# GeGLU feed-forward by seven block products: the order of the first loads and the shape of the last block

## Chip, cores and metric

The kernel runs on one core of one Trainium2 chip. The metric is device time in microseconds (us) of one execution. Three runs of the kernel before gave 272.92, 273.94 and 274.2 us; the median is 273.94. "Line" and L284 are lines of the kernel before unless said otherwise. TensorE (PE) does matmuls, with its weight loads shown apart (PEld); DVE, ACT and POOL are the vector, scalar and GpSimd engines; SP only issues DMAs and ACT issues some too (SPq and ACTq in the profile).

## The reference

```python
B, S, D, F = 32, 32, 1024, 3584
def reference(x, w_gate, w_up, w_down):
    return (_gelu(x @ w_gate) * (x @ w_up)) @ w_down
```

All inputs and the output are bf16; x is 1024 tokens by 1024 columns once its first two dimensions are flattened. `_gelu` is the tanh approximation.

## The kernel before, in words

Both matrix products are done on 2 x 2 blocks with seven block products instead of eight: sums and differences of blocks (s1 to s4 of the weights, t1 to t4 of x) are formed on POOL and DVE, multiplied on TensorE and combined. Tokens are split in two halves of 512 (NB), columns of x in two halves of four 128-wide pieces (KD = 4), columns of the gate and up weights in 28 pieces of 128 that are taken two at a time.

One of the seven products needs no sum: rows 512 to 1023 of w_gate (called `a12`) times the second column half of x for the first 512 tokens (`b21`, which has those x columns on partitions and the tokens along the row). The kernel begins with it, for 24 weight pieces "ahead", because it needs few bytes. `a12_ahead[i]` holds four weight pieces of group i, for the four 128-row steps k; `product_ahead` (line 284) multiplies one weight piece by `b21[:, k, cols]`, and its results wait in PSUM banks, for i = 0 in banks "CCAA".

The first x data does not come transposed. `load_nat` (line 197) loads x as it lies in memory, 128 tokens at a time, into `x_nat`: for column piece dt = 0 by SP's queue, for dt = 1 by ACT's queue. `transposed(dt)` (lines 260 to 267) makes four 128 x 128 transposes on TensorE (line 264), two to a PSUM tile, and DVE copies each pair to `b21` (line 267). Column pieces 2 and 3 come by a transposing DMA (`load_xT`, line 218). Gate rows k = 0 and k = 1 of group 0 come by SP's queue, one DMA each (line 211); those of group 1 by ACT's queue. Ahead of ACT's first load stands a tiny DMA `probe` (line 207) that nothing reads.

All of this is in a hand-written order (`manual_schedule`): every engine and every DMA queue works in program order. TensorE begins with six warm-up matmuls on constants (NWARM, line 256), then the four transposes of dt = 0, then products of k = 0 with the first 256 tokens, then `transposed(1)`, then k = 0 with the second 256 tokens, then k = 1 with both, then group 1:

```python
for k in range(KQ):                       # KQ = 2
    for half in range(2):
        for j in range(KB):               # KB = 4 weight pieces
            product_ahead(ps[0][j], 0, j, k, k + 1, slice(half * HALF * P, (half + 1) * HALF * P))
        if k == half == 0:
            transposed(1)
```

The second stage multiplies by w_down. Its products end with four stores of 128 rows (lines 577 to 581), after which one block is left: 128 tokens by 512 columns, the plain product of `a12_last` with `b21s` over 14 steps (HF). It is done as two blocks of 256 columns. Each is summed in a PSUM bank (line 588), added by DVE to `p1_last` (line 589) and stored by ACT's queue (line 590). The last of these stores ends the kernel.

Of the kernel before, what the change touches and what calls it, by code (L numbers as in the profile page):

```python
# [13 lines left out]
def kernel(  # L14
# [20 lines left out]
    nc = tc.nc  # L35
    P = nc.NUM_PARTITIONS
    fp32 = mybir.dt.float32
    f32r = mybir.dt.float32r
    bf16 = mybir.dt.bfloat16
# [4 lines left out]
    of = out.flatten_outer_dims()  # L44
    N, D = xf.shape
    F = w_gate.shape[1]
    NB = 512
    assert N == 2 * NB and D == 2 * NB and F % (4 * P) == 0
    DT, FT = D // P, F // P
    KD = DT // 2  # L50
# [4 lines left out]
    KQ = DT // 4  # L55
    HF = FT // 2
    MT = NB // P
    NWARM = 6
    KB = 4
    QF = HF // 2  # L60
    batches = [(0, KB), (KB, QF), (QF, QF + KB), (QF + KB, HF)]
# [2 lines left out]
    wg_r = w_gate.rearrange("(dt dp) f -> dp dt f", dp=P)  # L64
# [8 lines left out]
    xpool = one.enter_context(tc.tile_pool(name="x", bufs=1))  # L73
# [33 lines left out]
    def acc(tag):  # L107
        return ps1.tile([P, NB], fp32, name=f"ps{tag}", tag=tag, bufs=BANKS[tag])
# [5 lines left out]
    b21 = xpool.tile([P, KD, NB], bf16, name="b21")  # L114
# [72 lines left out]
    ones_w = nc.const_aps.tensor(1.0, [P, P], bf16)  # L187
    ones_m = nc.const_aps.tensor(1.0, [P, NB], bf16)
    ident = xpool.tile([P, P], bf16, name="ident")
    make_identity(nc, ident)  # L190
    NB_P = NB // P
    HALF = NB_P // 2
    x_nat = spool.tile([P, NB_P, KQ * P], bf16, name="x_nat", tag="s1")

    with tc.manual_schedule():
        def load_nat(eng, dt, p0, p1):
            eng.dma_start(  # L197
                out=x_nat[:, p0:p1, dt * P : (dt + 1) * P],
                in_=xf[p0 * P : p1 * P, (KD + dt) * P : (KD + dt + 1) * P].rearrange("(b p) d -> p b d", p=P),
            )  # L200

        assert KQ == 2
        load_nat(nc.sync, 0, 0, NB_P)


        probe = xpool.tile([P // 8, KQ, 2], bf16, name="probe")
        nc.scalar.dma_start(out=probe, in_=wg_r[::8, KD : KD + KQ, :2])

        def load_ahead(i, k0, k1, eng=nc.sync):
            f0 = i * KB  # L210
            eng.dma_start(
                out=a12_ahead[i][:, k0:k1, :],
                in_=wg_r[:, KD + k0 : KD + k1, f0 * P : (f0 + KB) * P],
            )

        def load_xT(nb, d0, d1):
            t = ((b11, b12), (b21, b22))[d0 // KD][nb]
            nc.sync.dma_start_transpose(
                out=t[:, d0 % KD : (d1 - 1) % KD + 1, :], in_=xf[nb * NB : (nb + 1) * NB, d0 * P : d1 * P]
            )  # L220

        load_ahead(0, 0, 1)
        load_nat(nc.scalar, 1, 0, NB_P)
        load_ahead(0, 1, 2)
        load_xT(0, KD + KQ, DT)
        load_ahead(1, 0, KQ, nc.scalar)
        a12_ahead += [spool.tile([P, KD, KB * P], bf16, name="a12b", tag=t) for t in ("s2", "s4", "s1", "s3")]
        for i in (0, 1):
            load_ahead(i, KQ, KD)
# [24 lines left out]
        warm_ps = acc("A")  # L254
        for _ in range(NWARM):
            nc.tensor.matmul(warm_ps, lhsT=ones_w, rhs=ones_m, start=True, stop=True)

        tps = [[ps1.tile([P, HALF * P], bf16, name="tp", tag="A", bufs=BANKS["A"]) for _ in range(2)] for _ in range(KQ)]

        def transposed(dt):  # L260
            for half, tp in enumerate(tps[dt]):
                p0 = half * HALF
                for b in range(HALF):
                    nc.tensor.transpose(  # L264
                        tp[:, b * P : (b + 1) * P], x_nat[:, p0 + b, dt * P : (dt + 1) * P], ident
                    )
                nc.vector.tensor_copy(b21[:, dt, p0 * P : (p0 + HALF) * P], tp)

        transposed(0)

        def prod(ps, lhs, rhs, start):
            for k in range(KD):
# [9 lines left out]
        def product_ahead(ps, i, j, k0=0, k1=KD, cols=slice(None)):  # L282
            for k in range(k0, k1):
                nc.tensor.matmul(  # L284
                    ps[:, cols],
                    lhsT=a12_ahead[i][:, k, j * P : (j + 1) * P],
                    rhs=b21[:, k, cols],
                    start=(k == 0 and not cols.start),
                    stop=(k == KD - 1),
                    skip_group_check=True,  # L290
                )
# [34 lines left out]
        ps = [[acc(t) for t in tags] for tags in ("CCAA", "AAAA")]  # L326
        for k in range(KQ):
            for half in range(2):
                for j in range(KB):
                    product_ahead(ps[0][j], 0, j, k, k + 1, slice(half * HALF * P, (half + 1) * HALF * P))  # L330
                if k == half == 0:
                    transposed(1)
        for j in range(KB):
            product_ahead(ps[1][j], 1, j, 0, KQ)
        for i in (0, 1):
# [28 lines left out]
        for ci in range(NCH):  # L364
# [8 lines left out]
            sn5, sn2, h1, h0 = [], [], [], []  # L373
# [17 lines left out]
            if fts[-1] < NAHEAD:  # L391
                h0 = first
# [184 lines left out]
        for m in range(MT):  # L577
            r0 = NB + m * P
            o = late.tile([P, NB], bf16, name="o_sb", tag="o_sb", bufs=2)
# [1 line left out]
            nc.scalar.dma_start(out=of[r0 : r0 + P, :NB], in_=o)  # L581

        o = late.tile([P, 2 * NB], bf16, name="o_last", tag="snb", bufs=MT)
        for h0 in range(0, NB, NB // 2):
            cols = slice(h0, h0 + NB // 2)
            ps = acc("C")[:, : NB // 2]
            for k in range(HF):
                nc.tensor.matmul(ps, lhsT=a12_last[:, k, :], rhs=b21s(k)[:, cols], start=(k == 0), stop=(k == HF - 1))  # L588
            tt(o[:, cols], p1_last[:, cols], ps, ADD)  # L589
            nc.scalar.dma_start(out=of[NB - P : NB, cols], in_=o[:, cols])  # L590
# [1 line left out]
_INS = ['x', 'w_gate', 'w_up', 'w_down']  # L592
_OUTS = [((32, 32, 1024), 'bfloat16')]
# [25 lines left out]
```

## Time and profile before

| what | value |
|---|---|
| median of three runs | 273.94 us |
| span of the profiled execution, first to last instruction | 272.0 us (272.05) |
| another time of the profiled execution | not given; the median is 1.89 us above its span |
| TensorE busy in the span | 267.1 us, 98% |
| first matmul of the warm-up | 0.78 us |
| first transpose of x / first product | 3.30 / 4.31 us |
| product of k = 1 begins | 6.28 us |
| last block: first matmul / last addition / end | 265.85 / 269.12 / 272.05 us |
| DMA, issue to landing: x_nat on SP / on ACT, 128 KB each | 2.5 / 3.2 us |
| probe / gate rows of 128 KB / of 256 KB on ACT | 2.1 / 3.0 and 4.4 / 4.6 us |
| stores of 128 KB / of 64 KB at the end | 1.7 / 1.6 us |

A row of the timeline has the start in us from the span's start, the duration, the engine with a "q" where its queue issues a DMA, the line, the operation, what it writes and reads, the shape, the number of instructions that the row merges, and in brackets the idle time before it with what ended it. A matmul's duration includes the time until its result is out, so that consecutive ones overlap: the pace is read from their starts.

### The profile page before, as it was taken

What the parts mean: (1) busy time and instruction counts of PE and PEld (TensorE: products, weight loads), DVE (VectorE), ACT (ScalarE), POOL (GpSimd) and SP (SyncE); (2) the same over time, 40 slices, a digit from 0 to 9 for tenths busy, and PEclk for the clock granted to TensorE, in tenths of its full rate; (3) what the DMA queues carried; (4) which work ended last, traced back from release to release, by engine and by line L of the source; (5) the groups of instructions that cost most, each with busy time, mean ns of one, the idle gap of its engine ahead of it and who ended that gap; (6) DMA issues with size and microseconds to landing.
All of it is one profiled execution on the core that took longest, in us unless ns stands there. A gap on an engine that the chain in (4) does not pass through costs nothing.

```text
span 272.0 us, 3399 instructions
## 1 busy us (share of the span) xinstructions
PE 267.1 (98%) x1199; PEld 193.4 (71%) x1212; DVE 201.2 (74%) x205; ACT 116.1 (43%) x189; POOL 119.3 (44%) x60
## 2 busy tenths in 40 slices
PE   8999999999999999999999999999999999999995
PEld 4444776886787688688688687764458888888884
DVE  1448998886976876876787458569999999997721
ACT  2335865545644643645636535434000307770000
POOL 1090099976995994994995978000000000000000
PEclk9999999999999999999999999999999999999999
DMA  7999130504505505415234290005981437855111
GB/s 174 323 227 281 39 99 17 158 25 130 154 2 154 154 4 154 128 27 157 69 88 118 50 319 17 0 2 182 356 273 60 158 112 253 276 187 174 54 61 58
DMA packets 56048, 35.86 MB, mean 132 GB/s; under 512 B 9824, under 2 KB 56032, under 8 KB 56032
## 3 DMA queue, kind: packets, MB, share of 16 engines
q1 hardware_dynamic: 52736, 33.17, 42.6%
q10 hardware_dynamic: 3296, 2.49, 2.9%
q8 instruction: 9, 0.15, 0.2%
q14 instruction: 7, 0.06, 0.1%
HBM read 31.72 MB, written 2.10 MB: 124 GB/s over the span
## 4 chain that ended last, share of the span: by engine, by line
PE 97%; DMA 1%; issue 0%; SPq 0%; DVE 0%
PE psA L273 38%; PE psA L425 24%; PE psC L273 19%; PE psC L425 7%; PE psA L284 5%; PE psC L284 3%; PE psC L588 1%; DMA a12a<-in_w_gate_dram 1%; SPq L197 0%; PE tp L264 0%; DVE o_last L589 0%
## 5 line engine op out<-in xcount | busy, mean ns | idle before, releaser
L273 PE MATMUL psA<-t,s 128*128 128x512 f32 x224 | 57.2, 397 | 0.0
L248 ACT ACTIVATE h<-c 128x512 bf16<-128x512 f32 x56 | 34.6, 631 | 41.6 <-DVE c L303 41.6
L273 PEld LDWEIGHTS psA<-t,s 128*128 128x128 f32 x224 | 42.1, 188 | 9.5
L170 POOL TENSOR_TENSOR s<-wu 128x1024 fp32r<-128x1024 bf16 x13 | 28.8, 2215 | 32.9 <-DMA wu<-in_w_up_dram 27.9
L171 POOL TENSOR_TENSOR s<-s,wg 128x1024 fp32r<-128x1024 f32 x14 | 31.7, 2263 | 15.0 <-DVE s L170 14.0
L173 POOL TENSOR_TENSOR s<-wg,wu 128x1024 fp32r<-128x1024 bf16 x13 | 28.4, 2188 | 0.0
L273 PE MATMUL psA<-b,wg 128*128 128x512 bf16 x119 | 27.8, 379 | 0.6
L273 PE MATMUL psA<-t,a22r 128*128 128x512 f32 x112 | 27.9, 391 | 0.0
L273 PE MATMUL psC<-t,s 128*128 128x512 f32 x112 | 27.9, 391 | 0.0
L273 PE MATMUL psC<-b22r,s 128*128 128x512 f32 x112 | 27.6, 389 | 0.0
L303 DVE TENSOR_TENSOR c<-sn,psA 128x512 f32<-128x512 f32 x32 | 21.8, 682 | 6.7 <-PE psA L273 5.7
L308 ACT COPY sn<-psC 128x512 f32<-128x512 f32 x28 | 16.4, 590 | 20.9 <-PE psC L273 15.2
L273 PEld LDWEIGHTS psC<-t,s 128*128 128x128 f32 x112 | 21.0, 188 | 4.5
L273 PEld LDWEIGHTS psA<-t,a22r 128*128 128x128 f32 x112 | 21.0, 188 | 4.5
L273 PEld LDWEIGHTS psC<-b22r,s 128*128 128x128 f32 x112 | 21.0, 188 | 4.4
L303 DVE TENSOR_TENSOR c<-sn,psC 128x512 f32<-128x512 f32 x28 | 19.2, 688 | 6.5 <-PE psC L273 6.5
L273 PEld LDWEIGHTS <-wg 128*128 128x128 bf16 x128 | 11.8, 98 | 15.3 <-issue 2.4
L172 POOL TENSOR_TENSOR s<-wg,s 128x1024 fp32r<-128x1024 bf16 x10 | 21.6, 2158 | 0.8
L402 DVE TENSOR_TENSOR lo<-c,h 128x512 bf16<-128x512 f32 x14 | 20.4, 1459 | 0.9
L308 ACT COPY sn<-psA 128x512 f32<-128x512 f32 x32 | 18.4, 592 | 6.1 <-PE psA L273 6.0
L303 DVE TENSOR_TENSOR c<-ahead,psA 128x512 f32<-128x512 f32 x24 | 16.4, 687 | 4.0 <-PE psA L273 2.4
L321 DVE TENSOR_TENSOR hi<-h,psA 128x512 bf16<-128x512 bf16 x14 | 9.6, 688 | 12.4 <-PE psA L273 12.4
(85 smaller groups left out, 381.0 us busy)
## 6 DMA issues: line engine op xcount, KB each, us to landing
wu<-in_w_up_dram SPq DMA_DIRECT2D x14, 512.0 KB, 4.0
wdb<-in_w_down_dram SPq DMA_DIRECT2D x12, 512.0 KB, 4.9
wg<-in_w_gate_dram SPq DMA_DIRECT2D x9, 512.0 KB, 5.2
wdb<-in_w_down_dram SPq DMA_DIRECT2D x12, 384.0 KB, 4.5
v<-in_w_down_dram SPq DMA_DIRECT2D x4, 512.0 KB, 6.4
out_dram<-o_sb ACTq DMA_DIRECT2D x15, 128.0 KB, 1.7
wg<-in_w_gate_dram SPq DMA_DIRECT2D x6, 256.0 KB, 4.6
v<-in_w_down_dram SPq DMA_DIRECT2D x4, 384.0 KB, 7.5
```

The lines of the kernel that those rows point to most:

```text
L170: yield engs[0].tensor_tensor(s1, a21, a22, ADD)
L171: yield engs[1].tensor_tensor(s2, s1, a11, SUB)
L172: yield engs[2].tensor_tensor(s4, a12, s2, SUB)
L173: yield engs[3].tensor_tensor(s3, a11, a21, SUB)
L248: nc.scalar.activation(h, src, ACT.Gelu_apprx_tanh)
L273: nc.tensor.matmul(ps, lhsT=lhs[:, k, :], rhs=rhs[:, k, :], start=(start and k == 0), stop=(k == KD - 1), skip_group_check=True,)
L284: nc.tensor.matmul(ps[:, cols], lhsT=a12_ahead[i][:, k, j * P : (j + 1) * P], rhs=b21[:, k, cols], start=(k == 0 and not cols.start), stop ...
L303: tt(t, s, ps, ADD)
L308: nc.scalar.copy(t, ps)
L321: tt(g_of(ft)[:, :NB], h0, psa, MUL)
L402: tt(g_of(ft)[:, NB:], added(sn5[fl], psa[fl]), h1[fl], MUL)
L425: nc.tensor.matmul(banks[m], lhsT=lhs(k)[:, m * P : (m + 1) * P], rhs=rhs(k), start=(start and k == 0), stop=(k == HF - 1), skip_group_che ...
```

## The change

At the start, x_nat for dt = 0 comes as two DMAs of two token blocks each, followed by dt = 1, all three on SP's queue. Gate rows k = 0 and k = 1 of group 0 go to ACT's queue, ahead of group 1's. The probe is gone. `transposed` now takes a half: only (0, 0) is done ahead of the first products; (0, 1), (1, 0) and (1, 1) follow them. There are five warm-up matmuls instead of six, and six small ones of 128 columns on constants (NFILL) behind the first two transposes.

At the end, the last block is done as 384 and 128 columns; the first is stored as before, and the second as two stores of 64 rows, one on ACT's and one on SP's queue.

```diff
-    NWARM = 6
+    NWARM = 5
+    NFILL = 6
...
-        load_nat(nc.sync, 0, 0, NB_P)
-        probe = xpool.tile([P // 8, KQ, 2], bf16, name="probe")
-        nc.scalar.dma_start(out=probe, in_=wg_r[::8, KD : KD + KQ, :2])
+        load_nat(nc.sync, 0, 0, HALF)
+        load_nat(nc.sync, 0, HALF, NB_P)
+        load_nat(nc.sync, 1, 0, NB_P)
...
-        load_ahead(0, 0, 1)
-        load_nat(nc.scalar, 1, 0, NB_P)
-        load_ahead(0, 1, 2)
+        for k in range(KQ):
+            load_ahead(0, k, k + 1, nc.scalar)
+        load_ahead(1, 0, KQ, nc.scalar)
         load_xT(0, KD + KQ, DT)
-        load_ahead(1, 0, KQ, nc.scalar)
...
-        def transposed(dt):
-            for half, tp in enumerate(tps[dt]):
-                p0 = half * HALF
-                for b in range(HALF):
-                    nc.tensor.transpose(
-                        tp[:, b * P : (b + 1) * P], x_nat[:, p0 + b, dt * P : (dt + 1) * P], ident
-                    )
-                nc.vector.tensor_copy(b21[:, dt, p0 * P : (p0 + HALF) * P], tp)
-
-        transposed(0)
+        def transposed(dt, half):
+            p0, tp = half * HALF, tps[dt][half]
+            for b in range(HALF):
+                nc.tensor.transpose(tp[:, b * P : (b + 1) * P], x_nat[:, p0 + b, dt * P : (dt + 1) * P], ident)
+            nc.vector.tensor_copy(b21[:, dt, p0 * P : (p0 + HALF) * P], tp)
+
+        transposed(0, 0)
+        for _ in range(NFILL):
+            nc.tensor.matmul(warm_ps[:, :P], lhsT=ones_w, rhs=ones_w, start=True, stop=True)
...
                 if k == half == 0:
-                    transposed(1)
+                    for dt, h in ((0, 1), (1, 0), (1, 1)):
+                        transposed(dt, h)
...
-        for h0 in range(0, NB, NB // 2):
-            cols = slice(h0, h0 + NB // 2)
-            ps = acc("C")[:, : NB // 2]
+        for h0, h1 in ((0, NB - P), (NB - P, NB)):
+            cols = slice(h0, h1)
+            ps = acc("C")[:, : h1 - h0]
             for k in range(HF):
                 nc.tensor.matmul(ps, lhsT=a12_last[:, k, :], rhs=b21s(k)[:, cols], start=(k == 0), stop=(k == HF - 1))
             tt(o[:, cols], p1_last[:, cols], ps, ADD)
-            nc.scalar.dma_start(out=of[NB - P : NB, cols], in_=o[:, cols])
+            if h1 < NB:
+                nc.scalar.dma_start(out=of[NB - P : NB, cols], in_=o[:, cols])
+                continue
+            for eng, r0 in ((nc.scalar, 0), (nc.sync, P // 2)):
+                eng.dma_start(
+                    out=of[NB - P + r0 : NB - P // 2 + r0, cols], in_=o[r0 : r0 + P // 2, cols]
+                )
```

## Prediction

> **What bounds the kernel now.** I read the busy table first, then the chain of waits, then the timeline of both ends. TensorE is busy 267.1 of 272.0 us, and the chain is TensorE for 97%.
>
> ```profile
> PE 267.1 (98%) x1199; PEld 193.4 (71%) x1212; DVE 201.2 (74%) x205; ACT 116.1 (43%) x189; POOL 119.3 (44%) x60
> ...
> PE 97%; DMA 1%; issue 0%; SPq 0%; DVE 0%
> ```
>
> The table by stretches says where the other 3% is: between 6.28 and 265.85 us TensorE's busy time falls short of the stretch by only 0.77 us (15.67 of 15.72, 37.83 of 38.00, 59.79 of 60.00, 59.76 of 60.00, 85.75 of 85.85, up to 265.85). So what is won or lost before 6.28 shifts all that follows, and what is won after 265.85 shortens the end. The change touches only these two stretches.
>
> The start, from the timeline (start, duration, engine, line; in brackets the idle time before it):
>
> ```profile
> 0.73 0.45 ACTq L207 DMA_DIRECT2D probe<-in_w_gate_dram  x1
> 0.74 0.45 SPq L197 DMA_DIRECT2D x_nat<-in_x_dram  x1
> 1.21 0.49 ACTq L197 DMA_DIRECT2D x_nat<-in_x_dram  x1
> 1.25 1.03 SPq L211 DMA_DIRECT2D a12a<-in_w_gate_dram  x2
> 1.73 0.53 ACTq L211 DMA_DIRECT2D a12a<-in_w_gate_dram  x1
> ...
> 3.30 0.62 PE L264 MATMUL tp<-ident,x_nat 128*128 128x128 bf16 x4
> 3.75 0.51 DVE L267 COPY b<-tp 128x256 bf16<-128x256 bf16 x2 [3.75 <-PE tp L264]
> 4.31 0.61 PE L284 MATMUL psC<-b,a12a 128*128 128x256 bf16 x2 [0.39 <-DMA a12a<-in_w_gate_dram]
> 5.14 0.63 PE L264 MATMUL tp<-ident,x_nat 128*128 128x128 bf16 x4
> 5.57 0.53 PE L284 MATMUL psC<-b,a12a 128*128 128x256 bf16 x2
> 6.28 0.39 PE L284 MATMUL psC<-b,a12a 128*128 128x256 bf16 x2
> ```
>
> Three waits can be seen: the first x piece (TensorE starts on it at 3.30), the first gate rows (0.39 us, until 4.31), and the second gate rows (the weight load at 6.28 waited 0.25 us, TensorE itself about 0.1). And the pace: warm-up weight loads start at 1.16, 1.58, 2.01, 2.44, that is 0.427 us for 512 columns; from 7.17 on 512 columns take 0.216 (32 in 7.07 us at 14.07). Narrow windows show the switch between 5.78 and 5.93. The granted-clock column reads 1.00 throughout, so the pace has to be read from the starts. I call it slow before about 5.86 and full after.
>
> The end:
>
> ```profile
> 265.85 3.23 PE L588 MATMUL psC<-wdb,a_last 128*128 128x256 bf16 x28
> 267.59 0.42 DVE L589 TENSOR_TENSOR o_last<-p_last,psC 128x256 bf16<-128x256 f32 x1 [2.44 <-PE psC L588]
> 268.05 1.87 ACTq L590 DMA_DIRECT2D out_dram<-o_last  x2
> 269.12 0.42 DVE L589 TENSOR_TENSOR o_last<-p_last,psC 128x256 bf16<-128x256 f32 x1 [1.11 <-PE psC L588]
> ```
>
> 28 matmuls, the last addition at 269.12, its store issued at 269.58, landed 1.6 us later (the rows of DMA issues), and then 0.8 us until the span ends, which the change does not touch.
>
> **The start, step by step.** Queues first. SP had x, gate row, gate row, transposed x; it gets x half, x half, x second piece, transposed x: four issues before and after, so its later loads keep their moments (the transposed x at 2.32). ACT had probe, x second piece, gate rows of the next group; it gets gate row, gate row, the same gate rows: again three, so its table load stays at 2.29. Only which bytes go first changes.
>
> (1) First x piece. 128 KB landed 2.5 us after issue (0.74 to 3.24); the probe, hardly any bytes, took 2.1. So 64 KB lands between 2.84 and 3.24; but now 128 KB of gate rows travels beside it, as beside the second x piece, which took 3.2: upper bound 3.94. I take 3.1, nearest to the first pair.
>
> (2) First gate row, issued at 0.73 rather than 1.25. It took 3.0 us then, so 3.7 at most; the wait of 0.39 us goes. What is late next is the transposed half. From the first transpose to the copy's start is 0.45 us (3.30 to 3.75), the copy itself 0.29, about 0.04 to TensorE: transposes at 3.14, half ready at 3.92. The six fillers are queued ahead on TensorE: two transposes and six fillers of 128 columns at 0.107 us (4 transposes: (0.63 - 0.31)/3) end at 3.14 + 8 x 0.107 = 4.00. So the first products start at 4.00 instead of 4.31: 0.31 us won, for now.
>
> (3) Four products of 256 columns at 0.213 end at 4.85. Then come six transposes where there were four: the second half's (0,1) was moved behind these products. End: 4.85 + 0.64 = 5.49. But the next products need (0,1)'s copy, a wait that was not there before (that copy was done at 4.25): 4.85 + 0.45 + 0.29 + 0.04 = 5.63. In the trace these products start at 5.57. So the 0.31 us is spent again: 0.10 on the two transposes and the rest of what it was ahead on the copy; queued behind that wait is all of TensorE.
>
> (4) From 5.63: two products at 0.213 and two at 0.109 (full pace past 5.86) end at about 6.20. The second gate row, issued at 1.21, takes at most the 4.4 us of its predecessor: 5.6, no wait. In the trace this point is 6.28. **Gain at the start: 0.08 us.** Ends: with x at 2.84 the point comes about 0.23 earlier; with x at 3.94 the new copy is ready at 6.47, and with four products at 0.109 the point is 6.9, 0.6 later.
>
> (5) The second x piece now is issued at 1.80 on SP, behind the two halves, instead of at 1.21. TensorE wants it at 4.85 + 0.21 = 5.06. By its own row (3.2 us) it lands at 5.0: no margin. The shortest of its size (2.5) gives 4.3. The longest is the gate row that had this very slot, issued at 1.80: 4.4 us, which gives 6.2. I take 5.0, since its company is what it was; at 6.2 TensorE would stand 1.2 us, the products begin at about 6.5 and end at 6.95: 0.65 us lost.
>
> The other loads: next group's gate rows, issued at 1.73 as before, landed at 6.3 and are wanted at 7.17; the transposed x landed at 7.2 and is wanted at 8.89. Covers of 0.9 and 1.7 us, if they slip; the change moves no byte in front of both queues together, only from one to the other. The missing probe and the one warm-up matmul fewer (0.43 us; TensorE then waits from 2.91 for x) cost nothing, as x is later than either.
>
> **The end.** The same 14 weight rows twice, 384 + 128 columns in place of 256 + 256. 256 columns take 0.109 us ((3.23 - 0.27)/27), 512 take 0.216, so 384 take 0.162: first block 14 x 0.162 = 2.27 instead of 1.53. The second block at full pace and 128 columns is not in the trace. Proportionally 0.056; if nothing is saved below the 256-column pace, 0.109; if weight loads of 98 ns (their row) don't overlap each other, 0.098. At slow pace loads of 0.15 us followed each other every 0.107 (the transposes), so they do overlap; the same ratio gives 0.098 x 0.107/0.15 = 0.070, which I take. Last matmul starts at 265.85 + 2.27 + 13 x 0.070 = 269.03 and ends 0.22 later (0.27 less half of 0.109): 269.25, against 269.08 before: +0.17. At 0.056 it is -0.02, at 0.098 +0.53, at 0.109 +0.67.
>
> The Trainium skill, "TensorE: Matmul & The Clock Gate", section "Back-to-back issue gap", puts a stream of load and matmul pairs at 128 columns at about 81 ns each. No row here shows it; by it the second block would cost 0.14 more than at 70 ns.
>
> The last addition: 512 columns 0.69, 256 columns 0.42, so 128 take 0.29: -0.13. DVE is free (the 384-column addition runs from about 268.33 for 0.55), ACT's queue too (first store issued by 269.25, the last wanted at 269.6). The last store: 128 KB 1.7 us, 64 KB 1.6, so 32 KB about 1.5: -0.1, with 0 and -0.2 as bounds, and above that +0.03 should SP issue slower (0.37 against 0.34). That the halves are on two queues I cost at nothing: an issue takes as long for 64 rows as for 128, as the probe's 16 rows took the same 0.45.
>
> The skill, "DMA: Bandwidth & Descriptors", section "Rules for kernel authors", speaks against it: two transfers to disjoint partition halves share the engines, so one should not bother. By it the term is that of one 32 KB store, as here.
>
> **Gain at the end: 0.17 - 0.13 - 0.1 = -0.06 us**, between -0.35 and +0.57. Sum: -0.08 - 0.06 = -0.14 us on a span of 272.05 us, hence 271.9. The page gives no other time of that execution; the median of the runs shown, 273.94, lies 1.89 above its span. I carry the difference over: **273.8 us**.
>
> **Rivals.** (a) Both ends at their good bounds (x at 2.84, 0.056 per matmul, short landing): -0.23 - 0.35, 273.4 us. For it: linear rows. (b) Weights hold the narrow block at 0.109: 274.3 us. The start's gain doesn't pay for it. (c) The pace switches earlier. TensorE stood from about 3.72 to 4.31 just before; the fillers cover that. Each us of slow pace costs half a us of work. Were the switch at 2.8 rather than 5.86, it would save up to 1.5: 272.3 us. Against it: in the trace 2.5 us of unbroken warm-up did not switch it. (d) The other side: the second x piece lands at 6.2 instead of 5.0. It decides from 5.06 on; the stall of 1.2 us costs 0.65, and being the longest idle stretch of the start, just before the switch, it may put that off. If TensorE needed another 5.1 us, as from 0.78 to 5.86, slow pace would last until 11.4 and cost 2.8; I take half of it, 1.4. With 0.65 and the end's gain: 275.9 us. For it: that slot did take 4.4 us.
>
> **Numbers.** Chances: forecast 0.56, (a) 0.09, (b) 0.09, (c) 0.13, (d) 0.13. Predicted 273.8. The range takes in (a), (b), (c) and the start's bound of +0.6 with the end's +0.57 (275.1), and leaves (d) out: 272.2 to 275.2. The runs shown spread over 1.28 us, so 0.5% (1.37 us) is about what can be told from no change. Faster by over 0.5%: 0.13; within: 0.74; slower: 0.13.
>
> **What would show it.** First product at about 4.0, not 4.31; the next half's products at about 5.6, waiting for DVE's copy; no wait for the second gate row; the last block's matmuls 0.07 apart; the last addition 0.29. Wrong, if a wait for x stands before the later transposes, if the pace switches elsewhere than near 5.9, or if the middle's shortfall of 0.77 us grows.

## The result, and the profile after

Eleven runs of the changed kernel took 275.19 us (median; 274.7 to 277.15), eleven of the kernel before 273.55 (272.92 to 275.38). The ratio is 1.0075, 95% interval 1.0054 to 1.0095: 0.75% slower, outside the 0.5% band and, with about 2 us in the mean, close to rival (d).

The times of the changed kernel fall in two groups: six from 274.7 to 275.19 (mean 275.03) and five from 276.46 to 277.15 (mean 276.84). Of the kernel before, ten lie between 272.92 and 274.2 (mean 273.62), one at 275.38. So the loss has two parts: the lower group moved up by 1.41 us, and the upper group, 1.8 us higher, became frequent: 5/11 x 1.8 - 1/11 x 1.8 = 0.65 us in the mean. Together 2.06 us.

The profiled execution is one of the lower group (275.09 us, span 273.30 against 272.05 before). The chain of waits on its page has a new member, x from memory:

```profile
PE 96%; DMA 2%; SPq 0%; DVE 0%; issue 0%
PE psA L270 38%; PE psA L423 24%; PE psC L270 19%; PE psC L423 7%; PE psA L281 5%; PE psC L281 2%; DMA x_nat<-in_x_dram 2%; PE psC L586 1%; SPq L198 0%; PE tp L261 0%; DVE o_last L587 0%
```

The timeline of the start (line 261 has the transposes, 281 the products, 266 the fillers):

```profile
0.74 1.49 SPq L198 DMA_DIRECT2D x_nat<-in_x_dram  x3
0.74 1.41 ACTq L210 DMA_DIRECT2D a12a<-in_w_gate_dram  x3
...
3.46 0.40 PE L261 MATMUL tp<-ident,x_nat 128*128 128x128 bf16 x2 [0.39 <-DMA x_nat<-in_x_dram]
3.64 0.85 PE L266 MATMUL psA<-const-bfloat16-1.0 128*128 128x128 bf16 x6
...
4.28 0.63 PE L281 MATMUL psC<-b,a12a 128*128 128x256 bf16 x2
...
4.96 0.28 PE L261 MATMUL tp<-ident,x_nat 128*128 128x128 bf16 x2
...
6.62 0.40 PE L261 MATMUL tp<-ident,x_nat 128*128 128x128 bf16 x4 [1.38 <-DMA x_nat<-in_x_dram]
...
7.29 0.38 PE L281 MATMUL psC<-b,a12a 128*128 128x256 bf16 x2
```

The first products start at 4.28 us (4.31 before), so nothing was won there. Then TensorE has done the two transposes of the second token half by 5.24 and stands until 6.62 for the second x piece: 1.38 us. The products of k = 1, at 6.28 before, start at 7.29: 1.01 us later. The last block starts at 266.83 instead of 265.85, 0.98 later, so the rest of the kernel hands the delay through. The DMA view of the first 14 us gives the landings (size, median us from issue to landing):

```profile
a12a<-in_w_gate_dram ACTq DMA_DIRECT2D x2, 128.0 KB, 2.5
a12a<-in_w_gate_dram ACTq DMA_DIRECT2D x1, 256.0 KB, 4.5
...
x_nat<-in_x_dram SPq DMA_DIRECT2D x2, 64.0 KB, 2.7
x_nat<-in_x_dram SPq DMA_DIRECT2D x1, 128.0 KB, 4.8
```

The second x piece took 4.8 us where it had taken 3.2, and was issued 0.55 us later (1.76 against 1.21). The gate rows, wanted later, came in 2.5 us.

The end, from the timeline:

```profile
266.83 3.23 PE L586 MATMUL psC<-wdb,a_last 128*128 128x384 bf16 x28
...
269.91 0.34 ACTq L589 DMA_DIRECT2D out_dram<-o_last  x1
270.10 0.29 DVE L587 TENSOR_TENSOR o_last<-p_last,psC 128x128 bf16<-128x128 f32 x1 [0.23 <-PE psC L586]
270.42 0.56 SPq L592 DMA_DIRECT2D out_dram<-o_last  x1
270.42 0.57 ACTq L592 DMA_DIRECT2D out_dram<-o_last  x1
```

Matmuls and addition are 0.13 us quicker: the last store is issued 3.59 us after the block's first matmul, where it was 3.72. But each of the two stores takes 0.56 us to issue instead of 0.34, and the last lands 2.0 us after issue instead of 1.6. First matmul of the last block to the end: 6.47 us, against 6.20. With 0.98 at the start, that is the 1.25 us between the two spans.

### The profile page after: what moved, and what is told of

Same layout as the page of the kernel before. It is cut to its first block, busy times and chain, and to the rows that moved or that the text cites. A ratio compares the mean times of both kernels' runs of the same rounds, so it can differ in the third digit from the quotient of the medians.

```text
span 273.3 us, 3425 instructions
## 1 busy us (share of the span) xinstructions
PE 267.5 (98%) x1217; PEld 193.1 (71%) x1217; DVE 201.7 (74%) x205; ACT 116.0 (42%) x189; POOL 119.3 (44%) x60
## 4 chain that ended last, share of the span: by engine, by line
PE 96%; DMA 2%; SPq 0%; DVE 0%; issue 0%
PE psA L270 38%; PE psA L423 24%; PE psC L270 19%; PE psC L423 7%; PE psA L281 5%; PE psC L281 2%; DMA x_nat<-in_x_dram 2%; PE psC L586 1%; SPq L198 0%; PE tp L261 0%; DVE o_last L587 0%
## 5 line engine op out<-in xcount | busy, mean ns | idle before, releaser
L270 PE MATMUL psA<-b,wg 128*128 128x512 bf16 x128 | 29.4, 380 | 0.0
```

Of the source, the lines that this page charges most:

```text
L270: nc.tensor.matmul(ps, lhsT=lhs[:, k, :], rhs=rhs[:, k, :], start=(start and k == 0), stop=(k == KD - 1), skip_group_check=True,)
```

## The experiments

Theory after this profile: at the start, the late second x piece alone makes the stall, the stall also makes the upper group of times frequent, and at the end the pair of stores is slow. Each ratio below is to the kernel before in the same series.

| kernel | median, us | ratio, 95% interval | runs in the upper group | k = 1 starts | last block to end |
|---|---|---|---|---|---|
| changed | 275.19 | 1.0075 (1.0054 to 1.0095) | 5 of 11 | 7.29 | 6.47 |
| e1 start only | 276.53 | 1.0088 (1.0057 to 1.0119) | 5 of 6 | 7.09 | 6.17 |
| e2 end only | 274.39 | 1.0025 (0.9998 to 1.0052) | 4 of 12 | 7.00 | 6.49 |
| e3 narrow block, one store | 273.45 | 0.9976 (0.9951 to 1.0001) | 0 of 12 | 6.60 | 5.89 |
| e4 equal blocks, two stores | 274.06 | 1.0019 (0.9992 to 1.0046) | 3 of 12 | 5.90 | 6.69 |
| e5 second x piece early | 274.05 | 0.9988 (0.9964 to 1.0012) | 1 of 12 | 5.95 | 6.18 |
| e6 256 KB moved away | 274.25 | 0.9993 (0.9968 to 1.0019) | 1 of 12 | 6.21 | 7.18 |
| e7 stall filled | 275.24 | 1.0040 (1.0016 to 1.0064) | 0 of 12 | 7.54 | 6.50 |
| e8 = e5 + e3 | 273.84 | 1.0003 (0.9984 to 1.0022) | 0 of 12 | 5.95 | 5.88 |
| e11 old start, wait filled | 273.47 | 0.9990 (0.9975 to 1.0005) | 0 of 12 | 5.95 | 6.22 |
| e13 = e11 + e3 | 273.21 | 0.9973 (0.9952 to 0.9993) | 0 of 12 | 6.11 | 5.91 |

The last two columns are us of one profiled execution each (e6's 7.18 has a last store that landed 2.6 us after its issue). The upper group is counted above 276 us where the start is the changed one with its late x piece (changed, e1, e7), above 275 elsewhere; e5's one run is 275.05. In the four series the kernel before had 5 of 29, 7 of 29, 2 of 23 and 2 of 17 runs above 275 us. e9, e10 and e12 were profiled once and are told by their rows.

### Which end: e1 and e2

e1 keeps the changed start and the old end; e2 the reverse. The edits are the two halves of the diff above.

> The changed start with the old end. Theory: the loss sits at the start, where the second x piece (128 KB, now third on SP's queue) lands at 6.57 us and TensorE stands 1.4 us in front of the last four transposes; the first products of k = 1 then start at 7.29 us instead of 6.28. If so, about +1.0 us in a profile with an early pace switch, 274.5 to 275.2 us as a median, and some runs 1.7 to 2 us above the others, as the changed kernel has them (five of eleven). Rival: the loss is at the end (two small stores); then this kernel is at 273.5 us and shows one group of times.

> The old start with the changed end. Theory: first matmul of the last block to the end of the span takes 6.47 us instead of 6.20: matmuls and addition win 0.13, the two small stores lose 0.40. So +0.3 us, about 273.8 us, in one group of times. Rival (start innocent, end guilty): +1 us or more.

The start carries the loss: e1 is 0.88% slower, five of its six runs in the upper group (276.34 to 276.92). In its profile, one of the lower group (275.15 us), x lands late again (issued at 1.75, the transposes start at 6.42) and k = 1 at 7.09; the median went past its bounds because of the upper group's share. e2's end is 6.49 us, +0.3 as expected; its time is not told apart from no change. One group of times was expected, and 4 of its 12 runs are in the upper one; the kernel before had 5 of 29 beside it.

e2's profile happened to be its slowest run, 276.1 us, and shows what an upper run is. The start is the old one; the rows are those of TensorE:

```profile
4.89 0.61 PE L284 MATMUL psC<-b,a12a 128*128 128x256 bf16 x2 [0.97 <-DMA a12a<-in_w_gate_dram]
...
7.42 0.64 PE L284 MATMUL psA<-b,a12a 128*128 128x256 bf16 x2
7.85 0.64 PE L284 MATMUL psC<-b,a12a 128*128 128x256 bf16 x2
```

Products of 256 columns start every 0.21 us still at 7.85, where in the profile before they went at 0.109 from about 5.86 on. Here a wait of 0.97 us stands before the first products, and the full pace comes after 9.4. In the changed kernel's profile the full pace is there at 4.86. No upper run with the changed start was profiled, so that those are late switches too is inferred from this one and from e7 below.

### Is the late x piece the cause, and why is it late: e5 and e6

```diff
 # e5: changed start, second x piece second on ACT's queue
-        load_nat(nc.sync, 1, 0, NB_P)
...
-        for k in range(KQ):
-            load_ahead(0, k, k + 1, nc.scalar)
-        load_ahead(1, 0, KQ, nc.scalar)
+        load_ahead(0, 0, 1, nc.scalar)
+        load_nat(nc.scalar, 1, 0, NB_P)
+        load_ahead(0, 1, 2, nc.scalar)
+        load_ahead(1, 0, KQ)
 # e6: changed start, only group 1's gate rows moved
-        load_ahead(1, 0, KQ, nc.scalar)
+        load_ahead(1, 0, KQ)
```

> The changed start with one move: the second x piece goes to ACT's queue, second, between the two gate rows (issued at about 1.2 us instead of 1.76), and the 256 KB of gate rows of the next group go to SP's queue in its place. TensorE's order (six transposes behind the first products, fillers) is the changed kernel's; the end is the old one. Theory (the late second x piece alone makes the loss): it lands at 4.4 to 5.3 us, TensorE waits for it at most 0.3 us, k = 1 starts at 6.1 to 6.5 us, median 273.4 to 274.2 us, mostly one group of times. Rival (halves and the new order of transposes on TensorE cost it): k = 1 still starts near 7 us and the median stays above 275 us.

> The changed start, but the 256 KB of gate rows of the next group leave ACT's queue and go to SP's, behind the second x piece, which keeps its place (third on SP, issued at about 1.76 us). Old end. If the second x piece is late because it shares the engines with those 256 KB, it lands by about 5.3 us, k = 1 starts by 6.6 us, median 273.5 to 274.3 us. If it is late because of its slot (issue 0.5 us later, behind the halves), it still lands after 6 us, and the median is 275 us or more.

Both have the old end. e5's x piece, issued at 1.19, lands at 4.15:

```profile
x_nat<-in_x_dram ACTq DMA_DIRECT2D x1, 128.0 KB, 3.0
```

Both edits take the loss away and leave TensorE's new order as it is: that order is not the cause. e6 also says why x is late. In the changed kernel 4.8 us, in e6 from the same slot (third on SP, 1.74 us):

```profile
x_nat<-in_x_dram SPq DMA_DIRECT2D x1, 128.0 KB, 3.4
```

The 256 KB of gate rows went from beside it to behind it, and it lands at 5.2 instead of 6.6. The transposing load behind x was thereby issued later too (2.80 instead of 2.27), so e6 alone does not tell these two apart. The changed kernel's own DMA view from 3.5 to 4.5 us, while x is on its way, does (q10 is ACT's queue, q1 SP's; packets, MB, share of the 16 engines):

```profile
q10 hardware_dynamic: 124, 0.12, 67.8%
q1 hardware_dynamic: 71, 0.02, 7.9%
```

In that microsecond the gate rows moved six times the bytes of all that stood on SP's queue, x and the transposing load together; in e6 SP's queue moved 0.20 MB in it. So x was slowed by its neighbour on the other queue, not by its slot. The Trainium skill, "DMA: Bandwidth & Descriptors", section "Queues, rings and completion order", says that each DMA engine takes turns between queues packet by packet. The runs show the slowing, not the turns, and why the shares were so unequal stays open.

### Does the stall bring the upper group: e7 and e11

```diff
 # e7: the changed kernel, TensorE kept busy in the stall
                     for dt, h in ((0, 1), (1, 0), (1, 1)):
                         transposed(dt, h)
+                        if (dt, h) == (0, 1):
+                            for _ in range(NSTALL):      # 12
+                                nc.tensor.matmul(ps[1][0][:, :P], lhsT=ones_w, rhs=ones_w, start=True, stop=True)
 # e11: the kernel before, its wait for the first gate row filled
         transposed(0)
+        for _ in range(NFILL):                           # 6
+            nc.tensor.matmul(warm_ps[:, :P], lhsT=ones_w, rhs=ones_w, start=True, stop=True)
```

> The changed kernel (both ends) with twelve more small matmuls of 128 columns on constants between the third and the fourth transposed half, where TensorE stands for the second x piece: about 1.3 us of work at the slow pace, 0.67 at the full one. Theory (the stall, beside its own 1 us, makes the switch to the full pace come later in about half of the runs, which costs those about 1.9 us): the stall itself stays, so the lower group stays at about 275 us, but the upper group (276.5 to 277.2, five of eleven runs) gets rare, at most two of ten or so. Rival (the two groups have another cause): the same share of runs near 277 us.

> The kernel before with six small matmuls on constants of 128 columns behind the first four transposes (0.64 us at the slow pace), where TensorE waits for the first gate row; nothing else changed. The kernel before has some runs near 276 us beside those near 273.8 (5 of 29, then 7 of 29). Theory (an idle stretch of TensorE in the first microseconds lets the switch come late): the runs near 276 become rare (at most one of twelve) and the lower group stays at 273.2 to 274.2 us. Rival (the late switch of the kernel before has nothing to do with that stretch): as many runs near 276 as before.

The twelve fillers stand behind the second of the four transposed halves. At the slow pace they last 1.3 us, about the stall; e7's profile is already at full pace there, where they cover 0.67, and TensorE still stands 1.20 us:

```profile
4.80 0.86 PE L334 MATMUL psA<-const-bfloat16-1.0 128*128 128x128 bf16 x12
6.87 0.40 PE L262 MATMUL tp<-ident,x_nat 128*128 128x128 bf16 x4 [1.20 <-DMA x_nat<-in_x_dram]
```

e7 keeps the late x and the lower group's time, 274.8 to 275.5, and not one of twelve runs is in the upper group, against 5 of 11 and 5 of 6 with the same start unfilled. The upper group thus comes from the idle stretch: when TensorE stands before the switch, the full pace often comes later. The Trainium skill, "TensorE: Matmul & The Clock Gate", section "What's actually happening", says that the clock is raised after a busy window of about 3.4 us that runs free of the kernel's start. By that page, an estimate, one missed window costs 3.4/2 = 1.7 us; the groups lie 1.8 us apart, and the profiles show the switch anywhere from before 4.5 us (e7) to 9.4 (e2). e11 has no upper run in twelve; the kernel before had only 2 of 23 beside it, so that agrees and shows little.

### Why the last store is slow: e3, e4, e9, e10, e12

All have the old start. The first theory was that two queues issuing at one moment disturb each other; rows of 256 bytes were the rival.

```diff
 # e3: 384 + 128 columns, one store
+            nc.scalar.dma_start(out=of[NB - P : NB, cols], in_=o[:, cols])
 # e4: 256 + 256 columns, the last as two stores
+        for h0, h1 in ((0, NB // 2), (NB // 2, NB)):
 # e9: both 64-row stores on ACT's queue
+            for eng, r0 in ((nc.scalar, 0), (nc.scalar, P // 2)):
 # e10: the last store whole, on SP's queue
+            (nc.scalar if h1 < NB else nc.sync).dma_start(out=of[NB - P : NB, cols], in_=o[:, cols])
 # e12: two stores of 128 rows by 64 columns
+            for eng, c0 in ((nc.scalar, h0), (nc.sync, h0 + P // 2)):
+                c = slice(c0, c0 + P // 2)
+                eng.dma_start(out=of[NB - P : NB, c], in_=o[:, c])
```

> The old start, the last block as 384 and 128 columns, its last store as one DMA of 128 rows on ACT's queue. Theory: the second queue or the number of stores makes the last store slow, so here it is issued in 0.34 us and lands about 1.6 us after issue: 6.07 us from the first matmul of the last block to the end, 0.13 below before. Rival: rows of 256 bytes make it slow; then it still lands 1.8 to 2.0 us after issue and the end is 6.3 to 6.5 us.

> The old start, the last block as 256 and 256 columns as before, its last store as two DMAs of 64 rows on ACT's and SP's queue (rows of 512 bytes). Theory (two queues at once make issue and landing slow): issue 0.56 us, landing about 2.0 us, end 0.4 us longer than before (6.6 us). Rival (rows of 256 bytes are the cause): issue 0.34, landing about 1.6, end 6.2 us as before.

> The old start, the last block as 384 and 128 columns, its last store as two DMAs of 64 rows, both on ACT's queue, one after the other. If two queues issuing at once make the last store slow, each is issued in about 0.34 us here and lands about 1.5 us after its issue; the end takes 6.2 us from the first matmul of the last block. If 64 rows (or 256-byte rows in small number) make it slow, an issue takes 0.56 us and the landing 1.8 to 2.0 here too, and the end 6.9 us.

> The old start, the last block as 384 and 128 columns, its last store as one DMA of 128 rows on SP's queue alone, nothing on ACT's at that moment. If simultaneity is the cause, SP issues it in about 0.34 to 0.37 us and it lands about 1.5 us after issue: the end takes 5.9 us, as with ACT. If SP's queue is the slow one, issue 0.56 us, landing 1.8 us, end 6.2 us.

> The old start, the last block as 384 and 128 columns, its last store as two DMAs of 128 rows by 64 columns, one on ACT's and one on SP's queue at the same moment. Two small stores on one queue (64 rows each) were issued in 0.54 and 0.60 us, so two queues at once is not needed for the slow issue. If 64 rows instead of 128 make it slow, each is issued in 0.34 to 0.37 us here and lands 1.4 to 1.6 us after issue, the end 5.9 us. If splitting one store into two makes it slow, whatever the rows, issue stays near 0.56 us, landing 1.8 us or more, end 6.3 us or more.

e3: one store of 128 rows with rows of 256 bytes is issued in 0.34 us and lands 1.46 after issue; the end takes 5.89 us. Rows of 256 bytes are not slow.

```profile
L590 ACTq DMA_DIRECT2D out_dram<-o_last x2: 338/338/339, 269.3 to 269.8; - x2
```

The 0.3 us at the end are not enough to tell e3's time from no change (0.9976, up to 1.0001). e4: with rows of 512 bytes the two stores are still slow, issue 0.56 and 0.57, landing 1.9 and 2.1, end 6.69. That looked like the two queues, but the theory fell with e9, where both stand on one queue (tile view of `o_last`: count, issue time in ns, minimum, median and maximum):

```profile
L594 ACTq DMA_DIRECT2D out_dram<-o_last x2: 541/570/598, 269.1 to 269.7; - x2
...
DMA to landing us min/median/max: 1.6/1.8/1.8
```

and with e12, two queues at the same moment but 128 rows each:

```profile
L595 SPq DMA_DIRECT2D out_dram<-o_last x1: 360/360/360, 268.9 to 268.9; - x1
L595 ACTq DMA_DIRECT2D out_dram<-o_last x1: 367/367/367, 268.9 to 268.9; - x1
```

It is the 64 rows that make the issue slow: 64-row stores take 0.54 to 0.60 us on either queue, alone or beside another; the last stores of 128 rows 0.34 to 0.37 on either queue (e10: SP 0.36, landing 1.48, end 5.92). What in a 64-row store costs this was not tried. e9's end is 6.95, as its expectation has it for 64 rows. e12's end is 6.11, not the 5.9 expected: its pair lands 1.5 and 1.7 us after issue, e3's single store 1.46. So of the 0.60 us between e2's end (6.49) and e3's (5.89), about 0.2 goes with there being two stores and 0.4 with their 64 rows, by one execution each.

### The parts put together: e8 and e13

> The two parts that measured no worse than before, together: the changed start with the second x piece second on ACT's queue and the next group's gate rows on SP's, and the last block as 384 and 128 columns with one last store of 128 rows on ACT's queue. Theory: the ends are independent, so k = 1 starts near 5.95 to 6.2 us (0.1 to 0.3 won), the end takes 5.9 us from the first matmul of the last block (0.3 won), and no run shows the late switch: 273.0 to 273.6 us, a ratio of 0.995 to 0.998 to the kernel before. Rival: the gains were scatter of the start; then 273.9 to 274.2.

> The kernel before with the six small matmuls behind its first transposes and with the last block as 384 and 128 columns and one last store: the two edits that each measured slightly below the kernel before. If they add up: end 5.9 us from the first matmul of the last block, no run near 276, median 273.1 to 273.5 us, ratio 0.995 to 0.998 with the interval below 1. If their gains were scatter: ratio 0.999 to 1.001.

e8, the repaired start with the good end, is no faster than before. Its profile shows one place where a gain at the start went: k = 1 starts at 5.95, 0.33 us earlier than in the profile before, but then TensorE waits for the other half of group 0's gate rows,

```profile
9.25 1.04 PE L281 MATMUL psC<-b,a12a 128*128 128x512 bf16 x4 [0.55 <-DMA a12a<-in_w_gate_dram]
```

issued at 3.72 and landed at 9.2 instead of 8.0. e5's profile has no such wait, and its lower group still is not below that of the kernel before: whether this happens in every run stays open. e13, the old loads with the wait filled and the narrow last block in one store, is faster than the kernel before, if by little: 273.21 us, 0.9973 (0.9952 to 0.9993). Part of it is that none of its runs is in the upper group, against 2 of 17 beside it.

## Why the prediction failed, point by point

- **What bounds the kernel**: right. A delay of 1.01 us at k = 1 was 0.98 at the last block.
- **The waits read from the profile before**: the first x piece was none. The sixth warm-up matmul starts at 2.86 and the next could start 0.427 us later, at 3.29; x had landed at 3.26, and the transposes started at 3.30.
- **Step (1), first x piece at 3.1 us**: it landed at 3.41 (2.7 us from issue, between the bounds 2.84 and 3.94). Half the bytes beside a gate row took longer than all of them beside the tiny probe (2.5).
- **Steps (2) and (3)**: the gate row stopped being the wait, and the fillers then set the first products (4.28, predicted 4.00; the 0.28 is step (1)'s). The full pace came at 4.86 in this execution. The copy of the second token half was done at 5.57 and x landed at 6.57, so the copy was not what came last. Where x is early, the wait of step (3) is there: in e5 TensorE stands 0.16 us for DVE's copy, until 5.52.
- **Step (4)** has a slip in its sum: two products at 0.213 and two at 0.109 from 5.63 end at 6.27, not 6.20, so the gain at the start would have been 0.01 and not 0.08. That did not decide the result.
- **Step (5) is the one that failed.** It gave the second x piece its old 3.2 us "since its company is what it was". Its company had changed: on the other queue there had been two gate rows of 128 KB; now there are 256 KB more, issued at 1.69, just before it. It took 4.8 us and landed at 6.57, beyond even the bound of 6.2; in e1 and e7 it took 4.6 and 5.1. e5 and e6 show that this alone makes the stall. The 3.2 us was thin ground besides: in the nine profiled executions with the old start the piece took 3.1 to 4.1. The same misreading stands in the sentence that no byte is put in front of both queues together: what counts is which bytes travel beside those that TensorE wants first.
- **Rival (d)** had the mechanism: x lands late, TensorE stands, the pace comes late. Sizes: stall 1.38 us for 1.2, k = 1 1.01 us later for 0.65; a late switch costs 1.8 us for 1.4, not in each run but in about half. It gave 275.9; the mean of the eleven runs is 275.85. That they meet so closely is luck: the stall and the end cost more than its terms and the late switch, over all runs, less (0.65 us against 1.4). What was wrong was its chance, 0.13, although the step had found no margin at all.
- **Rival (c)**, an earlier switch: in the profile the pace did come about 1 us earlier, yet in e1's, with the same start, it came only after 5.1, so this cannot be put down to the change.
- **The end, matmuls and addition**: 128 columns start every 0.056 us (14 of them from 269.12 to 269.85), the proportional bound, not 0.070, so the matmuls cost nothing where +0.17 was forecast; the addition took 0.29 as worked out. The 81 ns that the prediction cites from the Trainium skill, "TensorE: Matmul & The Clock Gate", section "Back-to-back issue gap", do not hold here. Without the split store this end is 0.3 us shorter (e3), the good bound of the prediction.
- **The end, last store**: "an issue takes as long for 64 rows as for 128" is wrong, 0.56 against 0.34, and the landing took 2.0 us instead of 1.5. The term -0.1 was +0.4. The probe of 16 tiny rows at the start was no price for it. The rule of the Trainium skill, "DMA: Bandwidth & Descriptors", section "Rules for kernel authors", that two partition halves are not worth the bother pointed the right way; the runs show a loss, which is more than the rule says.

## What to carry to other kernels

When loads are moved between queues, price each by what travels beside it until it lands, and let the bytes that the first engine wants next share the engines only with bytes that are wanted as early. Here an idle stretch in the first microseconds cost more than its length in about half of the runs, since the full pace came later; small matmuls in the wait took that part away (e7). Narrow the last store's columns and keep its 128 rows: the narrow block in one store made the end 0.3 us shorter in the profiles (e3, e8, e13), the same block in two stores of 64 rows made it 0.3 us longer.

## What was not expected of the hardware

- Stores of 64 rows took 0.54 to 0.60 us to issue and 1.8 to 2.1 to land in all five profiled executions that have them (changed, e2, e4, e7, e9). The last block's stores of 128 rows, with the same bytes or more, took 0.34 to 0.37 and 1.5 to 1.7, but for three that no run explains: two first stores with 0.71 (e5) and 0.67 us (e11) to issue and 1.9 to land, and e6's last one with 2.6 to land.
- The moment of the full pace differs between runs of one start: with the old loads it lies before 5.1 us in e3's profile and near 9.4 in e2's.
- Weight load and matmul pairs of 128 columns run at 0.056 us at full pace, a quarter of the 0.216 of 512 columns within 2 ns.
